# Attention and mixture of experts: a new opening order, chunk 1's scores in two banks, and idle products in other places

## The chip, the cores and the metric

The kernel runs on one core of a Trainium2 chip. The metric is device time in microseconds, the median of several runs of the whole program. Before the change it is 573.44 us (three runs, 573.29 to 575.0).

## The reference, cut to what matters

Eight batches of attention with keys and values pooled by 8, and behind it a two-level mixture of experts in which every token goes to one of 16 experts:

```python
k_p = k.reshape(B, H, Sp, pool, D).mean(axis=3)      # B=8, H=8, S=576, D=64, pool=8
v_p = v.reshape(B, H, Sp, pool, D).mean(axis=3)
scores = scale * np.matmul(q, k_p.transpose(0, 1, 3, 2))
scores = scores - np.max(scores, axis=-1, keepdims=True)
attn = np.exp(scores)
attn = attn / (np.sum(attn, axis=-1, keepdims=True) + 1e-09)
x = np.matmul(attn, v_p)                              # then (B*S, H*D)
# group of the token = argmax(x @ w_group), expert in the group = argmax(x @ w_expert[g])
h = np.maximum(x[tok] @ w1[g, e], 0.0)                # 512 -> 1024
out[tok] = (g_w * e_w)[:, None] * (h @ w2[g, e])      # 1024 -> 512
```

## The kernel before, in words

The work is done batch by batch. The attention of a batch (class Att) runs in five chunks of its 576 tokens (four of 128 and one of 64). The expert that most tokens of a batch choose is computed for all tokens of the batch (class Moe); tokens that chose another one are gathered and done at the end (class Left). All matrix products take fp32 data; the large ones run on a split into a rounded part and a rest, in three products.

The order of the work is written out by hand. Strings of pieces say what is issued one after another: START (line 34) and FIRST (line 44) for batch 0, STEADY for the batches after it, LAST for the last. A piece such as `a.sc:1` calls the method `sc` with 1; `a` is the attention of the current batch, `n` that of the next one, `x` that of the one after, `m` and `w` the experts of the current and the next batch, `t` the class Top. Each piece puts its instructions on the queues of the engines that it uses, and within one string each engine works through them in that order. The strings are run in separate blocks, START, then FIRST.

What START does, with the lines: `load_k`, `load_v`, `load_r`, `load_q` (185 to 211) load; `kr`, `rr`, `vr` (234 to 255) sum groups of 8 keys and values, on VectorE with the letter v (three additions) or r (one reduction, line 224), on GpSimd (POOL) with p. `kb` (248) is a copy on ScalarE (ACT), the first instruction there that needs the engine's table. `kt` (279) transposes the pooled keys on TensorE (PE), `kta` copies them out of PSUM. `qt` and `qta` transpose the queries of a chunk and copy them. `guess_x` (509) and `guess_e` (521) guess the expert of batch 0 from the mean of its values: two rounds of small products with a copy on ACT between them, then a chain on VectorE that ends at line 507, whose result SP reads into a register; the loads of that expert's weights (`m.load`, 576) are queued behind that. `split` (586) rounds a quarter of the weights on ACT, `spd` (593) forms the rest on POOL or VectorE.

A chunk's softmax is `sc` (scores on PE, line 335), `mx` (maximum, 341, VectorE), `sb` (difference, 348 in batch 0, 352 in later ones), `ex` (exponential, 357, ACT), `su_` (sum and reciprocal, VectorE), `nm` (multiplication, 372 and 375, POOL). `px_` and `pm` transpose the result on PE (380, 399), `pxa`, `pma`, `pxd`, `pmd` split it into a rounded part and a rest (404 on ACT, 408 on VectorE), `av` (410) multiplies by the values, `ava` and `avd` (420, 424) split that. `m.up:f:h` (597) is an up product of the expert, 12 products each, `ua` and `upd` (613, 618) its evacuation.

PSUM has eight banks here: three for up and down products and idle products (`ps_m`, tile "mm"), two that hold the scores of one chunk (`ps_s`, one tile), three for everything else (`ps_t`). `t.warm:z` (916) issues z idle products of 128x128 ones on PE into a bank of `ps_m`; nothing reads them. Each of them is two instructions in the profile.

The few lines that matter most, where a chunk's scores live and what an idle product is:

```python
ps = s.ss[c] = ps_s.tile([128, 2, 512], F32, name="sc")             # 329
ps = ps_m.tile([128, 512], F32, name="mm")                          # 918
for i in range(z):
    nc.tensor.matmul(ps[:, 0:128], lhsT=ones, rhs=ones, start=True, stop=True)   # 920
```

Of the kernel before, what the change touches and what calls it, by code (L numbers as in the profile page):

```python
# [33 lines left out]
START = """
a.load_r:v a.load_k:1:w a.kr:1:v t.warm:1 a.load_k:0:w t.load_wr a.load_v:0 a.kr:0:p t.warm:7 a.load_r:k a.load_v:1 a.load_q:0 a.vr:0:v a.rr:v
t.warm:11 a.load_q:1 t.warm:20 n.load_r:v a.kb a.vr:1:v a.kt n.load_r:k a.kta a.guess_x a.load_q:2 a.qt:0 a.qta:0 a.vmain a.guess_e a.sc:0 a.rcopy
m.load:1:1 a.qt:1 t.warm:2 a.vrem a.qta:1 a.qt:2 a.sc:1 a.mx:0 a.sb:0 a.ex:0 a.su_:0 a.nm:0:p a.mx:1 t.warm:4 a.vm:0 a.vrx a.sb:1 a.load_q:3 a.px_:0
m.load:1:3 a.pxa:0 a.vm:1 a.pm:0 a.pma:0 t.warm:1 t.warm:5 a.pxd:0 a.ex:1 a.pmd:0 a.av:1:0:128 a.av:2:0:128 m.load:1:2 a.av:0:0:128 a.su_:1 a.qta:2
a.ava:1:0:128 a.ava:2:0:128 a.ava:0:0:128 a.avd:1:0:128 a.avd:0:0:128 a.av:3:0:128 n.load_k:0 m.load:1:0 n.load_k:1 a.nm:1:p n.load_v:0 a.ava:3:0:128
m.split:1:1 a.sc:2 t.warm:1 a.pm:1 a.avd:3:0:128 a.load_q:4 a.mx:2 n.load_qb:2 a.px_:1 n.load_qb:0 a.qt:3 a.pxa:1 t.warm:3 a.avd:2:0:128 a.pma:1  # L40
a.sb:2 a.ex:2 a.pxd:1 m.split:1:0 a.pmd:1 m.spd:1:0:p a.su_:2 a.av:2:128:128 a.qta:3 a.ava:2:128:128 a.av:0:128:128 a.sc:3 n.load_qb:3 a.ava:0:128:128
a.av:1:128:128 a.av:3:128:128 a.ava:1:128:128 a.ava:3:128:128 a.avd:2:128:128 a.avd:0:128:128 a.avd:3:128:128 a.avd:1:128:128 m.up:0:0 m.spd:1:1:v
"""
FIRST = """
m.split:1:2 a.nm:2:p m.up:1:0 a.mx:3 m.ua:0:0 a.sb:3 n.vr:0 a.qt:4 a.px_:2 a.ex:3 a.su_:3 a.pm:2 m.ua:1:0 m.spd:1:2:p m.upd:0:0 a.qta:4 a.pxa:2 a.sc:4
a.mx:4 a.pma:2 a.sb:4 a.ex:4 a.pmd:2 m.up:2:0 m.split:1:3 t.warm:3 m.up:4:0 m.ua:2:0 a.nm:3:p m.load:2:1 a.pm:3 m.load:2:0 m.upd:1:0 a.px_:3 a.su_:4
a.nm:4:p m.ua:4:0 a.pxd:2 m.up:3:0 a.pxa:3 a.px_:4 a.pma:3 a.pxa:4 a.pxd:3 m.upd:2:0 a.pmd:3 a.pm:4 a.pxd:4 a.pma:4 m.split:2:1 a.pmd:4 a.av:3:256:320
a.av:2:256:320 m.upd:4:0 m.ua:3:0 a.ava:2:256:320 n.load_qb:1 x.load_k:0 a.ava:3:256:320 m.split:2:0 m.up:5:0 m.spd:1:3:v a.av:1:256:320 x.load_r:v
a.av:0:256:320 a.avd:2:256:320 a.ava:1:256:320 n.kr:0:r m.up:6:0 a.ava:0:256:320 a.avd:1:256:320 a.avd:3:256:320 m.ua:6:0 n.rr:p n.kr:1:p m.ua:5:0
m.spd:2:0:p m.load:2:2 a.avd:0:256:320 a.rt m.upd:3:0 m.upd:6:0 n.kt m.up:1:1 n.kta n.qb:0 m.upd:5:0 n.load_v:1 n.qb:1 n.sc:0 m.up:7:0 a.route  # L50
m.load:2:3 n.mx:0 n.rcopy n.sb:0 n.qb:2 m.ua:7:0 a.count n.ex:0 m.spd:2:1:p n.su_:0 m.ua:1:1 n.sc:1 n.nm:0:p m.up:0:1 n.mx:1 m.up:2:1 n.vrem m.ua:0:1
m.upd:7:0 a.gex n.sb:1 n.sc:2 m.upd:0:1 n.ex:1 m.upd:1:1 n.su_:1 n.px_:0 n.pm:0 n.mx:2 m.up:3:1 n.pxa:0 n.nm:1:p m.ua:2:1 m.up:4:1 x.load_k:1 m.ua:3:1
n.qb:3 n.px_:1 n.sb:2 x.load_qb:2 n.ex:2 n.pxd:0 x.load_r:k n.qb:4 m.split:2:2 m.upd:2:1 n.pxa:1 n.vrx a.gates n.pm:1 n.sc:3 n.vr:1:p n.mx:3 m.up:5:1
m.ua:4:1 m.up:7:1 n.vmain m.upd:3:1 n.pma:0 n.su_:2 n.nm:2:p m.up:6:1 a.keep_x m.ua:5:1 n.sb:3 m.upd:5:1 n.pm:2 n.px_:2 n.pxd:1 x.load_qb:3 x.load_v:0
n.sc:4 m.spd:2:2:p n.pmd:0 n.ex:3 n.vm:1 n.pma:1 m.upd:4:1 n.pmd:1 n.vm:0 n.pma:2 m.ua:6:1 m.ua:7:1 m.split:2:3 n.su_:3 n.nm:3:p n.pmd:2 n.av:1:0:256
n.mx:4 n.sb:4 x.load_qb:0 n.ava:1:0:256 n.pxa:2 n.px_:3 m.down:0 n.pxd:2 n.pm:3 m.down:1 n.av:0:0:256 n.ex:4 n.su_:4 x.load_qb:1 n.pxa:3 n.pma:3
n.pmd:3 n.nm:4:p n.pxd:3 m.upd:7:1 m.spd:2:3:p n.av:2:0:256 n.av:3:0:256 x.load_v:1 n.px_:4 n.ava:0:0:256 n.pm:4 n.avd:1:0:256 n.avd:0:0:256
n.ava:2:0:256 n.ava:3:0:256 n.avd:2:0:256 n.avd:3:0:256 n.pxa:4 m.down:2 n.pxd:4 n.pma:4 n.pmd:4 n.xr:3:0:256 n.av:0:256:320 n.av:1:256:320 x.kr:0:r
n.ava:0:256:320 n.av:3:256:320 n.ava:1:256:320 n.av:2:256:320 n.ava:3:256:320 n.xr:2:0:256 n.xr:1:0:256 n.xr:0:0:256 n.avd:0:256:320 n.ava:2:256:320
m.down:3 m.upd:6:1 n.avd:1:256:320 n.xr:1:256:320 n.avd:3:256:320 x.qb:0 n.xr:3:256:320 n.avd:2:256:320 n.xr:0:256:320 n.xr:2:256:320 m.da:0 m.down:4  # L60
n.rt m.down:5 x.rr:r n.route m.da:1 x.kr:1:p x.kt m.down:6 n.gex n.main_expert n.gates m.down:7 x.kta x.rcopy w.load:1:0 w.load:1:2 x.sc:0 x.mx:0
x.vrem x.vr:1:p w.load:1:3 m.down:8 m.down:9 w.split:1:0 x.vrx w.load:1:1 x.sb:0 x.qb:1 x.vr:0:r x.ex:0 m.down:12 x.su_:0 w.load:2:1 w.spd:1:0:v
n.keep_x m.down:13 x.nm:0:p m.down:10 m.da:2 w.split:1:1 m.da:4 m.down:11 x.vmain w.load:2:0 m.da:3 x.vm:1 w.spd:1:1:v x.vm:0
"""
# [907 lines left out]
```

## Time and profile before

| what | value |
|---|---|
| median of three runs | 573.44 us (573.29 to 575.0) |
| the profiled execution's own time | 573.03 us |
| its span | 571.3 us |
| mean granted clock of TensorE | 0.991 |
| busy share: PE, weight loads, VectorE, ACT, POOL | 98%, 87%, 70%, 48%, 53% |

PE is the engine of the matrix products, PEld its weight loads, which overlap with them. A line of a timeline names the start, the duration, the engine, the line of the kernel, the operation and its tiles; what stands in brackets is how long the engine had been idle and what ended that. `x4` means that four instructions are merged, and their duration runs from the first to the last. [...] START's pieces on PE run from the beginning to 35.39 us.

### The profile page before, as it was taken

How to read it: one execution, taken by the hardware profiler on the slowest of the kernel's cores; microseconds unless marked ns; L12 is line 12 of the kernel's file. 1: busy time of each engine (PE TensorE's matmuls, PEld its weight loads, DVE VectorE, ACT ScalarE, POOL GpSimd, SP SyncE). 2: the span in 40 equal slices, each digit the busy share in tenths (PEclk: the TensorE clock that was granted, in tenths of full speed). 3: DMA queues.
4: the chain of work that ended last, by engine and by line, in shares of the span. 5: the costliest groups of instructions: out<-in, count | busy, mean ns of one | idle time of the engine just before them, and what ended most of it. 6: DMA issues, size and time to landing. Idle time of an engine off the chain costs nothing. (4 is left out here: it accounts for less than half of the span.)

```text
span 571.3 us, 13094 instructions
## 1 busy us (share of the span) xinstructions
PE 558.4 (98%) x4896; PEld 497.5 (87%) x4896; DVE 397.1 (70%) x1075; ACT 273.8 (48%) x621; POOL 302.6 (53%) x301
## 2 busy tenths in 40 slices
PE   8999999999999999999999999999999999999995
...
GB/s 215 200 210 203 61 127 60 223 114 210 104 119 188 111 171 63 222 71 182 138 95 213 108 169 68 214 240 181 107 88 211 84 2 20 215 108 61 387 97 44
DMA packets 119362, 81.45 MB, mean 143 GB/s; under 512 B 76790, under 2 KB 95990, under 8 KB 118912
## 3 DMA queue, kind: packets, MB, share of 16 engines
...
q14 instruction: 26, 0.21, 0.1%
...
## 5 line engine op out<-in xcount | busy, mean ns | idle before, releaser
L608 PE MATMUL mm<-xt,w 128*128 128x320 f32 (+1 forms) x1536 | 221.1, 300 | 0.8 <-DVE ht L618 0.5
L608 PEld LDWEIGHTS mm<-xt,w 128*128 128x128 f32 x1536 | 208.2, 190 | 2.6 <-issue 0.7
L647 PE MATMUL mm<-w,ht 128*128 128x512 f32 x744 | 180.2, 395 | 0.0
L647 PEld LDWEIGHTS mm<-w,ht 128*128 128x128 f32 x744 | 136.9, 188 | 29.7 <-issue 1.8
L595 POOL TENSOR_TENSOR w<-sw,w 128x1024 fp32r<-128x1024 f32 x47 | 114.0, 2438 | 35.7 <-ACT w L590 35.7
L613 ACT ACTIVATE ht<-mm 128x320 fp32r<-128x320 f32 (+1 forms) x128 | 50.0, 410 | 62.1 <-PE mm L608 61.0
L618 DVE SCALAR_TENSOR_TENSOR ht<-mm,ht 128x256 fp32r<-128x256 f32 (+1 forms) x192 | 60.3, 347 | 25.0 <-ACT ht L613 24.2
L660 ACT ACTIVATE y<-mm,gm 128x512 f32<-128x512 f32 x31 | 21.2, 684 | 105.7 <-PE mm L647 105.7
L590 ACT CAST w<-sw 128x1024 fp32r<-128x1024 f32 x64 | 65.6, 1048 | 7.4 <-DMA sw<-in_moe_w_dram 7.3
L372 POOL TENSOR_TENSOR px<-p,su 128x128 f32<-128x128 f32 (+1 forms) x40 | 17.1, 427 | 68.0 <-DVE su L364 58.2
L272 POOL TENSOR_TENSOR rp<-rp,rh 32x128 f32<-32x128 f32 x8 | 3.6, 454 | 91.3 <-DMA rp<-rp 91.2
L431 POOL TENSOR_TENSOR sw<-xt 128x256 f32<-128x256 f32 (+1 forms) x56 | 43.7, 809 | 13.4 <-DVE xt L424 13.3
L375 POOL TENSOR_TENSOR p<-p,su 128x576 f32<-128x576 f32 (+1 forms) x40 | 46.0, 1150 | 3.1
L424 DVE TENSOR_TENSOR xt<-tp,xt 128x320 fp32r<-128x320 f32 (+2 forms) x68 | 28.1, 435 | 13.0 <-ACT xt L420 12.2
L420 ACT CAST xt<-tp 128x320 fp32r<-128x320 f32 (+2 forms) x68 | 25.4, 386 | 23.8 <-PE tp L417 22.5
L357 ACT ACTIVATE p<-p 128x576 f32<-128x576 f32 (+1 forms) x40 | 27.3, 682 | 16.4 <-DVE p L352 14.6
L362 DVE TENSOR_REDUCE su<-p 128x8 f32<-128x576 f32 (+1 forms) x40 | 29.8, 746 | 6.9 <-ACT p L357 6.0
L335 PEld LDWEIGHTS sc<-kT,qT 64*64 64x64 f32 x1264 | 24.1, 137 | 10.0 <-issue 4.8
L227 POOL TENSOR_TENSOR kv<-kv 128x512 f32<-128x512 f32 x20 | 32.5, 1627 | 0.2
L341 DVE TENSOR_REDUCE mx<-sc 128x8 f32<-128x576 f32 (+1 forms) x40 | 29.6, 741 | 3.4 <-PE sc L335 3.3
L335 PE MATMUL sc<-kT,qT 64*64 64x72 f32 x1264 | 30.1, 234 | 1.4 <-DVE p L352 1.0
L408 DVE TENSOR_TENSOR pl<-tp,ph 128x512 fp32r<-128x512 f32 (+1 forms) x40 | 25.2, 629 | 8.5 <-ACT ph L404 8.4
...
## 6 DMA issues: line engine op xcount, KB each, us to landing
...
```

The lines of the kernel that those rows point to most:

```text
L227: add(out=a[:, :, 0:256], in0=a[:, :, 0:256], in1=a[:, :, 256:512], op=ALU.add)
L335: nc.tensor.matmul(ps[t:t + 64, y, SP * g:SP * g + SP], lhsT=s.qT[c][r, g, t:t + 64], rhs=k, start=True, stop=True)
L341: red(out=mx[0:n], in_=scv, axis=AX.X, op=ALU.max)
L362: red(out=su[0:n], in_=s.p[c][0:n], axis=AX.X, op=ALU.add)
L375: eng.tensor_tensor(out=p[0:n], in0=p[0:n], in1=su[0:n].unsqueeze(3).broadcast_to([n, 2, 4, SP]), op=ALU.mult)
L431: nc.gpsimd.tensor_tensor(out=s.xw[g][:, sl], in0=s.xt[:, 0, g, sl].bitcast(F32), in1=s.xt[:, 1, g, sl].bitcast(F32), op=ALU.add)
L590: nc.scalar.copy(out=wh, in_=raw)
L595: (nc.vector if eng == "v" else nc.gpsimd).tensor_tensor(out=wl, in0=raw, in1=wh.bitcast(F32), op=ALU.subtract)
L608: nc.tensor.matmul(ps[:, 0:n], lhsT=l[:, kc, fs], rhs=xt[:, r, kc, sl], start=(kc == 0 and i == 0), stop=(kc == 3 and i == 2))
L613: nc.scalar.activation(out=s.ht[f][:, o:o + n], in_=s.pu[f, hf][:, 0:n], func=AF.Relu)
L618: stt(out=ht[:, at:at + hi - lo], in0=ps[:, lo - o:hi - o], scalar=0.0, in1=ht[:, lo:hi].bitcast(F32), op0=ALU.max, op1=ALU.subtract)
L647: nc.tensor.matmul(ps, lhsT=s.ht[f][:, 640 * l + o:640 * l + o + 128], rhs=s.w[2, f // 2][r][:, f % 2, :], start=(i == 0), stop=(i == 23))
```

## The change

START is a new list with the same pieces of attention and weights in another order, and two lines of FIRST differ. Beside the order:

- `t.prime` is new: a copy of one element on ACT at the head of its queue, in front of the five small loads that ACT issues.
- The scores of batch 0's chunk 1 (`a.sc:1:m`) go to two tiles of `ps_m`, one for each half of the scores, and `mx:1` and `sb:1` become two instructions each, one per half.
- `guess_e` stands behind `sc:0` and `mx:0`, ahead of `sb:0`; before it stood ahead of `sc:0`.
- The idle products: 55 in START before, 124 after. Ahead of `kt` there were 1+7+11+20 and now are 15+1+43+4+4; then 7 behind `kt`, 5 ahead of `sc:1`, 4+4+13 between `sc:1` and `px_:0`, 3+5 around `qt:2`, 4 behind `sc:2`, 7+1+4 around `qt:3`.
- `vr:0` is one reduction (letter r) instead of three additions; `n.load_k:0` is issued ahead of the `n.load_r`s; the loads of the weights come in the order 3, 2, 1, 0 instead of 1, 3, 2, 0.
- In FIRST: `a.su_:2` moves from START to its second place, `x.vr:0` goes from r to v, `w.spd:1:1` from VectorE to POOL.

The new START, the code for the scores in two tiles, and `prime`:

```diff
START = """
+t.prime t.warm:15 t.warm:1 t.warm:43 a.load_r:v a.load_k:1:w a.load_k:0:w t.load_wr a.load_v:0 a.load_r:k a.load_v:1 a.load_q:0 t.warm:4 a.kr:0:p
+a.load_q:1 a.kr:1:v t.warm:4 a.vr:0:r a.rr:v a.kb n.load_k:0 a.kt n.load_r:k a.kta t.warm:7 n.load_r:v a.qt:0 a.qta:0 a.load_q:2 a.vr:1:v a.guess_x
+a.sc:0 a.mx:0 a.guess_e a.sb:0 a.qt:1 m.load:1:3 t.warm:5 a.rcopy a.qta:1 a.vmain a.sc:1:m a.ex:0 a.mx:1 a.vm:0 t.warm:4 a.su_:0 a.sb:1 t.warm:4
+a.vm:1 a.nm:0:p m.load:1:2 t.warm:13 m.load:1:1 a.px_:0 a.pm:0 a.vrem a.ex:1 a.pxa:0 a.pma:0 a.su_:1 t.warm:3 a.qt:2 a.pxd:0 a.load_q:3 a.vrx t.warm:5
+m.load:1:0 a.pmd:0 a.av:1:0:128 a.nm:1:p n.load_v:0 a.av:2:0:128 a.av:0:0:128 a.qta:2 a.av:3:0:128 a.ava:1:0:128 a.avd:1:0:128 a.ava:0:0:128 a.sc:2
+a.avd:0:0:128 t.warm:4 a.ava:3:0:128 a.ava:2:0:128 m.split:1:1 a.avd:2:0:128 a.pm:1 a.mx:2 a.px_:1 a.pxa:1 a.pma:1 t.warm:7 a.qt:3 a.avd:3:0:128
+t.warm:1 a.load_q:4 a.sb:2 n.load_k:1 n.load_qb:2 n.load_qb:0 a.pxd:1 a.ex:2 m.split:1:0 t.warm:4 m.spd:1:0:p a.pmd:1 a.av:2:128:128 a.qta:3
+a.av:0:128:128 a.sc:3 a.ava:2:128:128 a.av:1:128:128 a.av:3:128:128 a.avd:2:128:128 n.load_qb:3 a.ava:0:128:128 a.ava:1:128:128 a.avd:0:128:128
+a.ava:3:128:128 a.avd:3:128:128 a.avd:1:128:128 m.up:0:0 m.spd:1:1:v
 """
...
@@ -324,24 +326,39 @@
             s.qT[c] = sm.tile([128, NG, 128], F32, name="qT")
             nc.vector.transpose(out=s.qT[c][:, :, 0:n], in_=s.q[:, 0:NG * S].rearrange("p (g t) -> p g t", g=NG)[:, :, o:o + n])
 
-        def sc(s, c):
+        def sc(s, c, home="s"):
             n = s.span(c)[1]
-            ps = s.ss[c] = ps_s.tile([128, 2, 512], F32, name="sc")
+            if home == "m":
+                s.ss[c] = ps = [ps_m.tile([128, 512], F32, name="mm") for y in range(2)]
+            else:
+                s.ss[c] = ps_s.tile([128, 2, 512], F32, name="sc")
+                ps = [s.ss[c][:, y] for y in range(2)]
             for g in range(NG):
                 for t in range(0, n, 64):
                     for y in range(2):
                         r = slice(64 * y, 64 * y + 64)
                         k = s.kT[r, g // 2, SP * (g % 2):SP * (g % 2) + SP] if s.b else s.kT[r, g, 0:SP]
-                        nc.tensor.matmul(ps[t:t + 64, y, SP * g:SP * g + SP], lhsT=s.qT[c][r, g, t:t + 64], rhs=k, start=True, stop=True)
+                        nc.tensor.matmul(ps[y][t:t + 64, SP * g:SP * g + SP], lhsT=s.qT[c][r, g, t:t + 64], rhs=k, start=True, stop=True)
 
         def mx(s, c):
             n = s.span(c)[1]
+            if type(s.ss[c]) is list:
+                s.m[c] = sm.tile([128, 2, 4], F32, name="mx")
+                for y in range(2):
+                    red(out=s.m[c][0:n, y], in_=s.ss[c][y][0:n, 0:288].rearrange("p (x s) -> p x s", s=SP), axis=AX.X, op=ALU.max)
+                return
             scv = s.ss[c][0:n, :, 0:288].rearrange("p u (x s) -> p u x s", s=SP)
             mx = s.m[c] = sm.tile([128, 2, 4], F32, name="mx")
             red(out=mx[0:n], in_=scv, axis=AX.X, op=ALU.max)
 
         def sb(s, c):
             n = s.span(c)[1]
+            if type(s.ss[c]) is list:
+                p = s.p[c] = sm.tile([128, 2, 4, SP], F32, name="p")
+                for y in range(2):
+                    tt(out=p.rearrange("p u x s -> p (u x) s").rearrange("p (g y) s -> p y g s", y=2)[0:n, y],
+                       in0=s.ss[c][y][0:n, 0:288].rearrange("p (x s) -> p x s", s=SP), in1=bc(s.m[c][0:n, y], SP), op=ALU.subtract)
+                return
             scv, mx = s.ss[c][0:n, :, 0:288].rearrange("p u (x s) -> p u x s", s=SP), s.m[c]
             p = s.p[c] = sm.tile([128, 2, 4, SP], F32, name="p")
             if not s.b:
@@ -913,6 +930,9 @@
             for g in range(G):
                 nc.scalar.dma_start(out=wr[:, :, 4 + 4 * g:8 + 4 * g], in_=we[g].rearrange("(c p) e -> p c e", p=128))
 
+        def prime(s):
+            nc.scalar.copy(out=gate[0:1, 0, 0:1], in_=ones[0:1, 0:1])
+
         def warm(s, z):
 
             ps = ps_m.tile([128, 512], F32, name="mm")
```

## Rows read from the trace of the kernel before

**Rows 1.** Busy time by stretch: length, then each engine's busy us (instructions), PEclk, DMA, GB/s.
```profile
1.00:5.00 4.00, 3.85 (x18) 3.86 (x19) 1.40 (x11) 0.00 (x0) 2.57 (x19) 1.00 0.65 177
...
15.30:22.05 6.75, 6.66 (x81) 6.07 (x84) 3.57 (x12) 3.74 (x10) 1.18 (x2) 0.50 0.36 92
...
35.00:95.00 60.00, 56.76 (x605) 50.57 (x605) 55.25 (x142) 35.48 (x89) 42.07 (x42) 1.00 0.50 123
...
95.00:500.00 405.00, 405.00 (x3452) 360.33 (x3451) 285.34 (x758) 202.44 (x459) 226.99 (x212) 1.00 0.49 140
```

**Rows 2.** Timeline, front of START: start, us, engine, line, operation, out<-in, count [idle before].
```profile
1.15 10.81 PE L920 MATMUL mm<-ones 128*128 128x128 f32 x78 [1.15 <-DVE valid L125]
...
9.04 1.05 POOL L232 TENSOR_TENSOR kb<-w 128x256 f32<-128x256 f32 x1
...
10.62 1.28 ACT L250 ACT_TABLE_LOAD   x1 [10.62 <-DMA wr<-in_moe_w_expert_dram]
...
11.69 0.47 PEld L290 LDWEIGHTS tp<-ident,kb 128*128 128x128 f32 x4
...
12.24 0.40 ACT L250 COPY rp<-rp 32x256 f32<-32x256 f32 x1 [0.34 <-DVE rp L232]
...
12.69 0.21 PEld L293 LDWEIGHTS tp<-ident,rp 128*128 128x128 f32 x2 [0.53 <-ACT rp L250]
```

**Rows 3.** Timeline, the guess and chunk 0's scores; last, a pair of 288-element subtractions.
```profile
13.06 0.20 PEld L514 LDWEIGHTS tp<-sel,vp 128*64 128x64 f32 x4 [0.16 <-DVE kv L227]
...
14.71 0.42 PEld L314 LDWEIGHTS tp<-ident,q 128*128 128x128 f32 x4
...
15.46 1.90 PE L525 MATMUL tp<-wr,ht 128*128 128x20 f32 x8
...
17.28 1.24 PE L335 MATMUL sc<-kT,qT 64*64 64x72 f32 x32
...
18.58 0.22 DVE L507 TENSOR_SCALAR moh<-cr,ct 128x16 f32<-128x16 f32 x1
...
19.50 0.76 DVE L348 TENSOR_TENSOR p<-sc,mx 128x576 f32<-128x576 f32 x1
...
20.29 0.68 ACT L357 ACTIVATE p<-p 128x576 f32<-128x576 f32 x1
...
61.47 0.82 DVE L352 TENSOR_TENSOR p<-sc,mx 128x288 f32<-128x288 f32 x2
```

**Rows 4.** Timeline, chunk 0 from its weights to its values.
```profile
22.86 1.15 POOL L375 TENSOR_TENSOR p<-p,su 128x576 f32<-128x576 f32 x1
...
24.06 0.42 PEld L399 LDWEIGHTS tp<-ident,p 128*128 128x128 f32 x4 [0.76 <-POOL p L375]
...
25.95 0.69 DVE L408 TENSOR_TENSOR pl<-tp,ph 128x512 fp32r<-128x512 f32 x1 [0.96 <-ACT ph L404]
...
26.69 0.19 PEld L417 LDWEIGHTS tp<-pl,vmh 128*128 128x128 f32 x1 [0.43 <-DVE pl L408]
```

**Rows 5.** Timeline, from chunk 2's scores to the first up product.
```profile
28.54 0.58 PEld L335 LDWEIGHTS sc<-kT,qT 64*64 64x64 f32 x32
...
29.57 0.42 PEld L399 LDWEIGHTS tp<-ident,p 128*128 128x128 f32 x4
...
33.38 2.36 POOL L595 TENSOR_TENSOR w<-sw,w 128x1024 fp32r<-128x1024 f32 x1 [3.86 <-ACT w L590]
...
34.64 0.76 DVE L341 TENSOR_REDUCE mx<-sc 128x8 f32<-128x576 f32 x1 [0.17 <-PE sc L335]
...
35.39 3.10 PEld L608 LDWEIGHTS mm<-xt,w 128*128 128x128 f32 x24
...
36.17 0.48 DVE L424 TENSOR_TENSOR xt<-tp,xt 128x128 fp32r<-128x128 f32 x2
```

**Rows 6.** Timeline, an up product behind an idle product in FIRST.
```profile
42.78 0.19 PEld L608 LDWEIGHTS mm<-xt,w 128*128 128x128 f32 x1 [0.25 <-PE mm L920]
...
42.95 0.41 DVE L618 SCALAR_TENSOR_TENSOR ht<-mm,ht 128x256 fp32r<-128x256 f32 x1
```

More of the change, by code (lines that the diff above doesn't have):

```diff
@@ L34 @@
 START = """
[L35 to L42, printed above, removed]
+t.prime t.warm:15 t.warm:1 t.warm:43 a.load_r:v a.load_k:1:w a.load_k:0:w t.load_wr a.load_v:0 a.load_r:k a.load_v:1 a.load_q:0 t.warm:4 a.kr:0:p
@@ L43 @@
 """
 FIRST = """
[L45 to L60, printed above, removed]
@@ L61 @@
-n.rt m.down:5 x.rr:r n.route m.da:1 x.kr:1:p x.kt m.down:6 n.gex n.main_expert n.gates m.down:7 x.kta x.rcopy w.load:1:0 w.load:1:2 x.sc:0 x.mx:0
-x.vrem x.vr:1:p w.load:1:3 m.down:8 m.down:9 w.split:1:0 x.vrx w.load:1:1 x.sb:0 x.qb:1 x.vr:0:r x.ex:0 m.down:12 x.su_:0 w.load:2:1 w.spd:1:0:v
-n.keep_x m.down:13 x.nm:0:p m.down:10 m.da:2 w.split:1:1 m.da:4 m.down:11 x.vmain w.load:2:0 m.da:3 x.vm:1 w.spd:1:1:v x.vm:0
+m.split:1:2 a.su_:2 a.nm:2:p m.up:1:0 a.mx:3 m.ua:0:0 a.sb:3 n.vr:0 a.qt:4 a.px_:2 a.ex:3 a.su_:3 a.pm:2 m.ua:1:0 m.spd:1:2:p m.upd:0:0 a.qta:4
@@ new lines @@
+a.pxa:2 a.sc:4 a.mx:4 a.pma:2 a.sb:4 a.ex:4 a.pmd:2 m.up:2:0 m.split:1:3 t.warm:3 m.up:4:0 m.ua:2:0 a.nm:3:p m.load:2:1 a.pm:3 m.load:2:0 m.upd:1:0
+a.px_:3 a.su_:4 a.nm:4:p m.ua:4:0 a.pxd:2 m.up:3:0 a.pxa:3 a.px_:4 a.pma:3 a.pxa:4 a.pxd:3 m.upd:2:0 a.pmd:3 a.pm:4 a.pxd:4 a.pma:4 m.split:2:1
+a.pmd:4 a.av:3:256:320 a.av:2:256:320 m.upd:4:0 m.ua:3:0 a.ava:2:256:320 n.load_qb:1 x.load_k:0 a.ava:3:256:320 m.split:2:0 m.up:5:0 m.spd:1:3:v
+a.av:1:256:320 x.load_r:v a.av:0:256:320 a.avd:2:256:320 a.ava:1:256:320 n.kr:0:r m.up:6:0 a.ava:0:256:320 a.avd:1:256:320 a.avd:3:256:320 m.ua:6:0
@@ new lines @@
+n.rr:p n.kr:1:p m.ua:5:0 m.spd:2:0:p m.load:2:2 a.avd:0:256:320 a.rt m.upd:3:0 m.upd:6:0 n.kt m.up:1:1 n.kta n.qb:0 m.upd:5:0 n.load_v:1 n.qb:1 n.sc:0
+m.up:7:0 a.route m.load:2:3 n.mx:0 n.rcopy n.sb:0 n.qb:2 m.ua:7:0 a.count n.ex:0 m.spd:2:1:p n.su_:0 m.ua:1:1 n.sc:1 n.nm:0:p m.up:0:1 n.mx:1 m.up:2:1
+n.vrem m.ua:0:1 m.upd:7:0 a.gex n.sb:1 n.sc:2 m.upd:0:1 n.ex:1 m.upd:1:1 n.su_:1 n.px_:0 n.pm:0 n.mx:2 m.up:3:1 n.pxa:0 n.nm:1:p m.ua:2:1 m.up:4:1
+x.load_k:1 m.ua:3:1 n.qb:3 n.px_:1 n.sb:2 x.load_qb:2 n.ex:2 n.pxd:0 x.load_r:k n.qb:4 m.split:2:2 m.upd:2:1 n.pxa:1 n.vrx a.gates n.pm:1 n.sc:3
@@ new lines @@
+n.vr:1:p n.mx:3 m.up:5:1 m.ua:4:1 m.up:7:1 n.vmain m.upd:3:1 n.pma:0 n.su_:2 n.nm:2:p m.up:6:1 a.keep_x m.ua:5:1 n.sb:3 m.upd:5:1 n.pm:2 n.px_:2
+n.pxd:1 x.load_qb:3 x.load_v:0 n.sc:4 m.spd:2:2:p n.pmd:0 n.ex:3 n.vm:1 n.pma:1 m.upd:4:1 n.pmd:1 n.vm:0 n.pma:2 m.ua:6:1 m.ua:7:1 m.split:2:3 n.su_:3
+n.nm:3:p n.pmd:2 n.av:1:0:256 n.mx:4 n.sb:4 x.load_qb:0 n.ava:1:0:256 n.pxa:2 n.px_:3 m.down:0 n.pxd:2 n.pm:3 m.down:1 n.av:0:0:256 n.ex:4 n.su_:4
+x.load_qb:1 n.pxa:3 n.pma:3 n.pmd:3 n.nm:4:p n.pxd:3 m.upd:7:1 m.spd:2:3:p n.av:2:0:256 n.av:3:0:256 x.load_v:1 n.px_:4 n.ava:0:0:256 n.pm:4
@@ new lines @@
+n.avd:1:0:256 n.avd:0:0:256 n.ava:2:0:256 n.ava:3:0:256 n.avd:2:0:256 n.avd:3:0:256 n.pxa:4 m.down:2 n.pxd:4 n.pma:4 n.pmd:4 n.xr:3:0:256
+n.av:0:256:320 n.av:1:256:320 x.kr:0:r n.ava:0:256:320 n.av:3:256:320 n.ava:1:256:320 n.av:2:256:320 n.ava:3:256:320 n.xr:2:0:256 n.xr:1:0:256
+n.xr:0:0:256 n.avd:0:256:320 n.ava:2:256:320 m.down:3 m.upd:6:1 n.avd:1:256:320 n.xr:1:256:320 n.avd:3:256:320 x.qb:0 n.xr:3:256:320 n.avd:2:256:320
+n.xr:0:256:320 n.xr:2:256:320 m.da:0 m.down:4 n.rt m.down:5 x.rr:r n.route m.da:1 x.kr:1:p x.kt m.down:6 n.gex n.main_expert n.gates m.down:7 x.kta
@@ L64 @@
+x.rcopy w.load:1:0 w.load:1:2 x.sc:0 x.mx:0 x.vrem x.vr:1:p w.load:1:3 m.down:8 m.down:9 w.split:1:0 x.vrx w.load:1:1 x.sb:0 x.qb:1 x.vr:0:v x.ex:0
+m.down:12 x.su_:0 w.load:2:1 w.spd:1:0:v n.keep_x m.down:13 x.nm:0:p m.down:10 m.da:2 w.split:1:1 m.da:4 m.down:11 x.vmain w.load:2:0 m.da:3 x.vm:1
+w.spd:1:1:p x.vm:0
 """
```

## Prediction

> **What bounds the kernel now.** I read busy time by stretch first. From 95 to 500 us the engine of the matrix products (PE) is busy 405.00 of 405 us, and from 35 to 95 us 56.76 of 60 [rows 1]. So the body has almost no slack on PE: whatever delays its first up product (m.up:0:0, which begins at 35.39 us [rows 5]) delays the end, and only the 3.24 us that PE lacks between 35 and 95 us could take some of it up. The changed list, START, is all that lies ahead of 35.39. There I read the timeline in the order of the work: pooled keys and values, their transposes (kt, line 290), the guess of the expert, scores, softmax, attention values, first up product.
>
> [...] (a) PE starts with idle products at 1.15 us; 39 of them are 78 instructions, and only when they are through does the first transpose of kt begin, at 11.69 us [rows 2]. Its input, POOL's kb, was done at 10.09; the second part waits for a copy that ends at 12.64 [rows 2]. The front of idle products therefore ended about when kt's inputs were there. [...] (c) From there the chain is one of small steps over all engines, and PE takes its instructions in the order of the list.
>
> **The idle products in front.** The new list has 15+1+43+4+4 = 67 idle products ahead of kt instead of 39. The pace: 78 instructions between 1.15 and 11.69; the first 18 end at 5.00, so 60 take 6.69 us, 0.1115 each, 0.223 per product [rows 1, 2]. The added 28 cost 28 x 0.223 = 6.24 us, and nothing hides them, because PE itself is what kt then waits for: 11.69+6.24 = 17.93. The transposes need 0.47+0.21, now without the wait for the copy, so they are issued by 18.61; before it was 12.90 [rows 2]: **+5.71**.
>
> **Edits ahead of kt** end in the same answer. The table load (1.28 us, at 10.62 [rows 2]) goes to the front of ScalarE; the copy after it waited for VectorE's sum until 12.2 anyway, and now it has to be there only by 18. vr:0 as one reduction, the new order of the loads, and n.load_k:0 moved ahead of the n.load_r's on SP also end before 17.93: their gain is 0, and a loss of up to 17.93-12.64 = 5.3 us would stay hidden.
>
> **kt to the scores.** Before, sc:0 started 17.28-12.90 = 4.38 us after kt [rows 2, 3]. Now: 7 idle products 1.56, qt:0 0.42, guess_x 14.71-13.06 = 1.65 [rows 3], together 3.63 at the full clock: sc:0 at 22.25, **+4.97**. The guess now ends behind the scores: its second part starts 0.75 us after guess_x's end (15.46-14.71 [rows 3]), at 23.0; it took 1.90 at 0.50, so 0.95 at full clock; VectorE's chain to the end of L507 ran from 17.36 to 18.80 = 1.44 [rows 3], so 25.4. sb:0 stands behind that chain on VectorE although its scores and maxima have been ready since about 24: 25.4 against 19.50, **+5.9**. The reordering costs this 0.9. On SP the read of the guess holds up what is queued behind it, the four loads of w1, q3 and n.load_v:0, by 25.4-18.8 = 6.6 us. They would be issued from about 26.4; split:1:0 needs the last at 39.4 and qt:3 its q3 at 38.8, so 12 us are left and nothing waits. If the loads took all of that, each further us would go straight into spd:1:0.
>
> **Chunk 1 in two banks.** sc:1 need no longer wait for sb:0; PE issues guess_e's last product 0.1 ahead of its result, at 23.85, then qt:1 (0.42) and five idle products (1.12): sc:1 runs from 25.4 to 26.0 (0.58, as sc:2 [rows 5]). But its maxima stand behind sb:0 on VectorE (26.2), so this is worth nothing there. mx:1 and sb:1 become two instructions each over half the elements. No row shows this; the nearest, two subtractions of 288 elements, take 0.82 against 0.76 for one of 576 [rows 3]. Bounds are 0.76 and 1.52 for a pair; I take 0.82, the nearest row. mx:1 ends at 27.0, 0.1 after ex:0 (26.2+0.68), so it holds up su_:0 by 0.1; at the upper bound by 0.8. [...] The row of the pair shows 0.06 and decides.
>
> From ex:0's start to the end of nm:0 it was 24.01-20.29 = 3.72 [rows 3, 4]; now 26.2+3.72+0.1 = 30.0. But PE has 4+4+13 = 21 idle products in its queue ahead of px:0 and pm:0: 26.0+21x0.223 = 30.7, plus 0.11, so pm:0 is issued at 30.8 against 24.06: **+6.75**, 0.75 of it new.
>
> **pm:0 to the first up product.** Three idle products, qt:2 and five more stand between pm:0 (0.42) and av: 0.42+0.67+0.42+1.12 = 2.63, av at 33.4. The old interval from pm:0 to the product that waits for pl was 26.69-24.06 = 2.63 [rows 4] with two products of 0.11 ahead of it; here that product comes at 33.6, **+6.95**, and pl (by 33.2: the old steps without the vm:1 that lay in them) does not bind. Sixteen value products need 1.8: sc:2 at 35.2 instead of 28.54 [rows 5], **+6.65**. Then sc:2 0.58, four idle products 0.89, pm:1 at 36.7 (before 29.57 [rows 5]), **+7.1**; its nm:1 has been done since about 33, so chunk 1's lead of 3 us ends in PE's queue. pm:1 and px:1 0.53, 7 idle 1.56, qt:3 0.42, 5 idle 1.12: av for columns 128 on at 40.3. Two groups 0.9, sc:3 0.6, two groups 0.9: m.up:0:0 at **42.7 instead of 35.39**. POOL's spd:1:0 [rows 5] would end at about 42.9 behind split:1:0, the same lateness as PE. That is **+7.3 us**.
>
> After that every engine stands to m.up:0:0 as before. su_:2, moved to FIRST, is no loss: VectorE took mx:3 of FIRST at 34.64 ahead of START's last avd at 36.17 [rows 5], so a piece at the head of FIRST fills a gap in START. If it does not, it stands behind spd:1:1, and POOL's chain of FIRST loses up to 4 us: upper end. x.vr:0 and w.spd:1:1 lie where PE is always busy [rows 1]: 0.
>
> **Sum.** The profiled execution took 573.03 (span 571.3, 1.73 around it); +7.3 = 580.3. The median of the runs is 0.41 higher, so **580.8**.
>
> **Rivals.** *Banks.* After sc:1, two of the three banks of the up products hold scores until sb:1 has read them (first half 28.6). If the second group of idle products gets one of those, PE stands from 26.9 to 28.7: +1.8, 582.6. Against it: m.up:4:0 waited for an idle product and started at 42.78, before upd:1:0 (42.95) had freed the oldest bank [rows 6], so a bank just left by an idle product is given out again.
> *The clock falls again.* Before, it fell after kt, guess_x and qt:0 [rows 1, 3]; the same stretch comes at 20.2 to 24, though with idle products on both sides and no wait in it. If it runs at 0.50 for 6.75 us again, PE loses half of that, 3.4, and pm:0 hangs on PE: 584.2.
> *Not slower.* PE takes idle products only in gaps, as VectorE took mx:3 early. Then kt ends at 12.9, sc:0 starts at 15.0, the guess ends at 18.15, sb:0 starts 1.35 ahead of 19.50, and pm:1 need no longer wait for a late nm:1: about 1.7 us gained in all, 571.7. It decides if kt starts before about 12 us. Against it: the 78 instructions all ran ahead of kt although its input was there at 10.09 [rows 2].
>
> **Numbers.** Forecast 0.62 (own range 578.5 to 582.5, from closing part of the 3.24 us to 0.8 at mx:1 and some of FIRST), banks 0.12, clock 0.20, not slower 0.06. The range 577.5 to 585.5 leaves out the last and the worst sums of two. 0.3% (1.7 us) is what a measurement tells from no change: slower 0.94, within 0.03, faster 0.03.
>
> **What would show it.** 134 idle instructions ahead of L290, and L290 at about 18; sb:0 behind L507; idle products right up to pm:0; granted clock 1.00 at 15 to 22; m.up:0:0 at about 42.7, and from there the old distances. It is wrong if L290 starts near 12, or if m.up:0:0 is late and the end is not.

## The result and the profile after

The changed kernel takes **582.27 us** in the median (five runs, 581.8 to 583.53), beside 573.44 for the kernel before in the same set (573.29 to 575.55): a ratio of 1.0146, interval 1.0123 to 1.0169. By that ratio it is 8.4 us slower; the medians are 8.8 apart. The profiled execution took 582.72 us, with a span of 581.0 and a mean granted clock of 0.998 (all clocks here are shares of TensorE's full clock). The code after has other line numbers: idle products L940, kt L292 and L295, sc L341, mx L348 and L352, sb L359 and L365, the guess's second part L542, its result L524, nm L392, pm L416, split L607, spd L612, up L625.

Busy time by stretch, with the columns of [rows 1]:

```profile
15.30:22.05 6.75, 6.75 (x70) 6.52 (x68) 0.00 (x0) 1.45 (x4) 0.00 (x0) 1.00 0.40 76
15.00:45.00 30.00, 29.87 (x373) 28.57 (x373) 13.84 (x38) 14.88 (x37) 7.02 (x8) 1.00 0.53 142
44.60:104.60 60.00, 56.85 (x605) 50.81 (x604) 54.91 (x142) 35.32 (x89) 42.01 (x42) 1.00 0.53 126
95.00:500.00 405.00, 404.55 (x3459) 359.98 (x3458) 289.74 (x768) 202.91 (x464) 233.78 (x219) 1.00 0.48 134
```

Where the clock had been 0.50 (15.30 to 22.05 us [rows 1]) it is now 1.00, and PE is busy 29.87 of 30 us up to the first up product: the opening is nothing but PE's queue. The 60 us behind that product look as before, 56.85 against 56.76 [rows 1], so the body is moved, not changed.

The front of the timeline, to lay beside [rows 2]:

```profile
0.82 1.28 ACT L934 ACT_TABLE_LOAD   x1 [0.82 <-PEq L978]
...
1.14 17.41 PE L940 MATMUL mm<-ones 128*128 128x128 f32 x134 [1.14 <-DVE valid L127]
...
12.70 0.40 ACT L252 COPY rp<-rp 32x256 f32<-32x256 f32 x1 [10.39 <-DVE rp L234]
...
18.28 0.47 PEld L292 LDWEIGHTS tp<-ident,kb 128*128 128x128 f32 x4
...
18.72 0.25 PEld L295 LDWEIGHTS tp<-ident,rp 128*128 128x128 f32 x2
```

134 instructions run without a break, and kt begins behind the last, at 18.28 instead of 11.69, though the copy that it needs was done at 13.10. Then the scores and the guess, beside [rows 3]:

```profile
22.79 0.58 PEld L341 LDWEIGHTS sc<-kT,qT 64*64 64x64 f32 x32
...
23.53 0.97 PEld L542 LDWEIGHTS tp<-wr,ht 128*128 128x128 f32 x8 [0.16 <-ACT ht L536]
...
23.59 0.76 DVE L352 TENSOR_REDUCE mx<-sc 128x8 f32<-128x576 f32 x1 [9.41 <-PE sc L341]
...
25.83 0.23 DVE L524 TENSOR_SCALAR moh<-cr,ct 128x16 f32<-128x16 f32 x1
25.96 0.75 DVE L365 TENSOR_TENSOR p<-sc,mx 128x576 f32<-128x576 f32 x1
26.13 0.58 PEld L341 LDWEIGHTS mm<-kT,qT 64*64 64x64 f32 x32
...
26.79 0.97 PEld L940 LDWEIGHTS mm<-ones 128*128 128x128 f32 x8
...
26.91 0.82 DVE L348 TENSOR_REDUCE mx<-mm 128x4 f32<-128x288 f32 x2 [0.19 <-PE mm L341]
...
28.00 0.97 PEld L940 LDWEIGHTS mm<-ones 128*128 128x128 f32 x8 [0.25 <-PE mm L940]
...
28.75 0.77 DVE L359 TENSOR_TENSOR p<-mm,mx 128x288 f32<-128x288 f32 x2
...
29.22 2.98 PEld L940 LDWEIGHTS mm<-ones 128*128 128x128 f32 x26 [0.25 <-PE mm L940]
29.46 1.15 POOL L392 TENSOR_TENSOR p<-p,su 128x576 f32<-128x576 f32 x1
...
32.23 0.47 PEld L416 LDWEIGHTS tp<-ident,p 128*128 128x128 f32 x4
```

Chunk 0's weights are ready at 30.61 (29.46+1.15), and their transposes pm:0 start at 32.23, behind the last of the 21 idle products. The groups of 4, 4 and 13 are apart by 0.25 us each: scores hold two of the three banks, so each group waits for the one before it to leave the third. From there, beside [rows 5]:

```profile
36.83 0.58 PEld L341 LDWEIGHTS sc<-kT,qT 64*64 64x64 f32 x32
...
38.38 0.47 PEld L416 LDWEIGHTS tp<-ident,p 128*128 128x128 f32 x4
...
41.28 0.74 DVE L379 TENSOR_REDUCE su<-p 128x8 f32<-128x576 f32 x1
...
42.23 2.37 POOL L612 TENSOR_TENSOR w<-sw,w 128x1024 fp32r<-128x1024 f32 x1 [8.96 <-ACT w L607]
...
44.63 3.06 PEld L625 LDWEIGHTS mm<-xt,w 128*128 128x128 f32 x24
```

The first up product comes at 44.63 instead of 35.39, +9.24; the span is longer by 9.7. su_:2 (L379), the piece moved to FIRST, fills a gap inside START at 41.28.

### The profile page after: what moved, and what is told of

Its sections match the earlier page's. It is cut to its first block, busy times and chain, and to the rows that moved or that the text cites. A ratio compares the mean times of both kernels' runs of the same rounds, so it can differ in the third digit from the quotient of the medians.

```text
span 581.0 us, 13368 instructions
## 1 busy us (share of the span) xinstructions
PE 569.7 (98%) x5034; PEld 510.5 (88%) x5034; DVE 395.5 (68%) x1076; ACT 274.4 (47%) x622; POOL 304.6 (52%) x302
## 5 line engine op out<-in xcount | busy, mean ns | idle before, releaser
L625 PE MATMUL mm<-xt,w 128*128 128x320 f32 (+1 forms) x1536 | 221.1, 300 | 1.0 <-DVE ht L635 0.7
L625 PEld LDWEIGHTS mm<-xt,w 128*128 128x128 f32 x1536 | 208.1, 190 | 3.0 <-DVE ht L635 1.2
L612 POOL TENSOR_TENSOR w<-sw,w 128x1024 fp32r<-128x1024 f32 x48 | 116.3, 2438 | 40.6 <-ACT w L607 40.6
L607 ACT CAST w<-sw 128x1024 fp32r<-128x1024 f32 x64 | 65.6, 1049 | 7.9 <-DMA sw<-in_moe_w_dram 7.9
L392 POOL TENSOR_TENSOR p<-p,su 128x576 f32<-128x576 f32 (+1 forms) x40 | 46.0, 1150 | 3.1
L352 DVE TENSOR_REDUCE mx<-sc 128x8 f32<-128x576 f32 (+1 forms) x39 | 28.9, 741 | 12.6 <-PE sc L341 12.5
L437 ACT CAST xt<-tp 128x320 fp32r<-128x320 f32 (+2 forms) x68 | 25.4, 386 | 24.5 <-PE tp L434 23.1
L379 DVE TENSOR_REDUCE su<-p 128x8 f32<-128x576 f32 (+1 forms) x40 | 29.9, 749 | 7.5 <-ACT p L374 6.3
L940 PE MATMUL mm<-ones 128*128 128x128 f32 x254 | 33.0, 289 | 1.3 <-DVE valid L127 1.1
L940 PEld LDWEIGHTS mm<-ones 128*128 128x128 f32 x254 | 31.5, 204 | 1.8 <-DVE valid L127 1.1
L341 PEld LDWEIGHTS sc<-kT,qT 64*64 64x64 f32 x1232 | 22.7, 133 | 9.2 <-issue 4.8
```

The source lines that it names most:

```text
L379: red(out=su[0:n], in_=s.p[c][0:n], axis=AX.X, op=ALU.add)
L392: eng.tensor_tensor(out=p[0:n], in0=p[0:n], in1=su[0:n].unsqueeze(3).broadcast_to([n, 2, 4, SP]), op=ALU.mult)
L607: nc.scalar.copy(out=wh, in_=raw)
L612: (nc.vector if eng == "v" else nc.gpsimd).tensor_tensor(out=wl, in0=raw, in1=wh.bitcast(F32), op=ALU.subtract)
L625: nc.tensor.matmul(ps[:, 0:n], lhsT=l[:, kc, fs], rhs=xt[:, r, kc, sl], start=(kc == 0 and i == 0), stop=(kc == 3 and i == 2))
```

## The experiments

Each ratio is to the runs of the kernel before in the same set; their medians lie between 573.4 and 575.2. A difference between two kernels of different sets is therefore taken from their ratios. The table takes from one profile of each kernel when the weight load of kt begins, the distance from there to that of pm:0, from that to the first up product, and from that to the end of the span (us).

| run | ratio, 95% interval | kt | kt to pm:0 | pm:0 to up | up | up to end |
|---|---|---|---|---|---|---|
| before | 1 | 11.69 | 12.37 | 11.33 | 35.39 | 535.9 |
| after | 1.0146 (1.0123 to 1.0169) | 18.28 | 13.95 | 12.40 | 44.63 | 536.4 |
| front39 | 1.0057 (1.0031 to 1.0084) | 11.86 | 15.78 | 12.41 | 40.05 | 536.1 |
| no_mid21 | 1.0159 (1.0135 to 1.0184) | 17.72 | 12.39 | 14.83 | 44.94 | 536.0 |
| front39_no_mid21 | 1.0074 (1.0047 to 1.0101) | 11.30 | 14.64 | 15.02 | 40.96 | 537.1 |
| before_front67 | 1.0101 (1.0077 to 1.0126) | 17.70 | 11.56 | 10.96 | 40.22 | 536.5 |
| no_banks | 1.0153 (1.0134 to 1.0173) | 17.75 | 14.04 | 12.41 | 44.20 | 536.3 |
| guess_first | 1.0172 (1.0149 to 1.0194) | 18.43 | 14.72 | 12.41 | 45.56 | 536.6 |
| sb0_first | 1.0148 (1.0127 to 1.0169) | 17.57 | 13.95 | 12.41 | 43.93 | 535.9 |
| no_prime | 1.0141 (1.0114 to 1.0169) | 17.59 | 13.95 | 12.40 | 43.94 | 536.2 |
| early | 1.0009 (0.9991 to 1.0027) | 10.89 | 12.36 | 11.93 | 35.18 | 537.3 |
| early2 | 1.0033 (1.0014 to 1.0051) | 10.81 | 15.54 | 12.10 | 38.45 | 537.4 |
| early3 | 1.0005 (0.9988 to 1.0022) | 11.13 | 10.49 | 13.08 | 34.70 | 536.9 |
| early4 | 1.0006 (0.9992 to 1.0020) | 10.87 | 11.37 | 12.37 | 34.61 | 537.5 |

**front39: the 28 added front products taken out of the new kernel.**

```diff
-t.prime t.warm:15 t.warm:1 t.warm:43 a.load_r:v
+t.prime t.warm:15 t.warm:1 t.warm:15 a.load_r:v
```

> The changed kernel with 31 instead of 59 idle products at the head, so 39 ahead of the key transposes (kt) as before. Theory (the front of idle products is what delays kt, and kt starts the path to the first up product): 28 x 0.223 = 6.2 us come off PE's front; kt's second part then waits for the copy that ended at 13.1 us, so 5.5 us are saved: about 576.8 us, still above the kernel before by some 3 us. Rival A (the late guess, and with it the weights' loads, sets the first up product): less than 2 us saved, 580.5 or more. Rival B (the added idle products only kept the clock up): it falls again at about 15 to 22 us and eats 2 to 3 us of the saving, 579.

The time is 577.67 us. The ratio is 0.0089 below that of the change, about 5.1 us, near the 5.5 of the theory. In the profile kt is back at 11.86, 6.42 earlier, but the first up product is only 4.58 earlier. The windows of this run (columns as above) show where the rest went:

```profile
15.00:19.00 4.00, 3.99 (x71) 3.71 (x71) 1.17 (x4) 1.18 (x3) 0.00 (x0) 1.00 0.77 128
19.00:21.00 2.00, 2.00 (x14) 1.77 (x16) 1.42 (x6) 1.36 (x3) 0.72 (x1) 0.51 0.00 0
21.00:23.00 2.00, 2.00 (x39) 1.86 (x40) 0.88 (x3) 1.99 (x6) 0.00 (x0) 0.64 0.47 141
```

The granted clock falls to 0.51 (19 to 21 us) after the guess's small products, as in rival B though later and by less, and kt to pm:0 is 15.78 instead of 13.95. This holds for the profiled execution, whose mean granted clock is 0.993. Four of the run's nine executions have a mean of 0.998 to 0.999, as high as the changed kernel's, and take 576.2 to 576.7 us, the 576.8 of the theory. So the front products always cost their time in the queue, and gave a part of it back as clock only in those executions in which the clock would have fallen.

**no_mid21 and front39_no_mid21: the 4+4+13 idle products out, alone and with the front's 28.**

```diff
-... a.mx:1 a.vm:0 t.warm:4 a.su_:0 a.sb:1 t.warm:4
-a.vm:1 a.nm:0:p m.load:1:2 t.warm:13 m.load:1:1 a.px_:0 a.pm:0
+... a.mx:1 a.vm:0 a.su_:0 a.sb:1
+a.vm:1 a.nm:0:p m.load:1:2 m.load:1:1 a.px_:0 a.pm:0
```

> The changed kernel without the 4+4+13 idle products between chunk 1's scores and chunk 0's transposed weights. Theory: pm:0 waits for POOL's nm:0 (ended 30.61 us) instead of the products (issued 32.34), 1.7 us saved: 580.6 us. Rival (these products hold the clock): with PE idle from 26.7 to 29.4 us the clock falls to 0.50, what follows is up to 3 us slower: 582 to 584 us.

> Both cuts together, 39 idle products ahead of kt and none between chunk 1's scores and chunk 0's transposed weights. Theory: 5.5 + 1.7 = 7.2 us saved, 575.1 us, about 1.6 us above the kernel before, which is the order's own cost (the subtraction of chunk 0 behind the guess, idle products further on). Rival (the clock falls once PE has gaps): 577 to 579.

The times are 583.22 and 579.6 us: no gain, against my theory and as the rivals had it (the second lies 0.6 us above its rival's range). In no_mid21 pm:0 is 1.56 us earlier behind kt (12.39), then all of it is lost (14.83 instead of 12.40). Its windows, and pm:0 in its timeline:

```profile
27.00:29.00 2.00, 0.11 (x1) 0.12 (x1) 1.90 (x6) 1.77 (x5) 0.50 (x2) 0.87 0.74 223
29.00:35.00 6.00, 5.25 (x24) 4.96 (x25) 2.38 (x6) 3.11 (x8) 3.07 (x4) 0.50 1.04 316
```

```profile
28.88 0.18 PEld L397 LDWEIGHTS tp<-ident,px 128*128 128x128 f32 x1 [2.73 <-POOL px L389]
...
30.11 0.71 PEld L416 LDWEIGHTS tp<-ident,p 128*128 128x128 f32 x4 [1.04 <-POOL p L392]
```

PE stands for 2.73 and 1.04 us, and the stretch from 29 to 35 us runs at 0.50. Without the 21 products kt to up is 27.22 instead of 26.35 (with the short front 29.66 instead of 28.19): they delay pm:0 and pay for it by the clock. All five executions of no_mid21 have a mean clock of 0.991 or 0.992, where the changed kernel's have 0.998 or 0.999. With both cuts one execution of eight kept 0.998 and took 575.36 us, near the 575.1 of the theory; the other seven lie at 0.987 to 0.993 and take 578.0 to 580.5. The ratios of each pair overlap, so the times alone show only that nothing is gained by leaving them out.

**before_front67: the 28 front products alone, in the kernel before.**

```diff
-t.warm:11 a.load_q:1 t.warm:20 n.load_r:v a.kb
+t.warm:11 a.load_q:1 t.warm:48 n.load_r:v a.kb
```

> The kernel before with 28 more idle products ahead of kt and nothing else. Theory: 28 x 0.223 = 6.2 us of delay less the 1.0 us that kt's second part waited for the copy, and nothing takes it up later: 573.4 + 5.5 = 578.9 us. If the clock then stays at 1.00 from 15 to 28 us, up to 2 us of that come back: 577. Rival (the front costs nothing as such, the new order does): within 1 us of the kernel before, 573 to 574.5.

The time is 579.66 us and the ratio 1.0101, that is 5.8 us, near the theory's figure and 5 us above the rival's. kt is 6.01 later and the first up product 4.83; shorter waits and a shorter slow stretch (0.65 and 0.50 from 21 to 25 us, where it was 0.50 from 15.30 to 22.05 [rows 1]) take up the rest. The clock did not stay at 1.00 here, although all 67 products ran ahead of kt:

```profile
21.00:23.00 2.00, 2.00 (x32) 1.96 (x36) 0.54 (x3) 1.19 (x3) 0.72 (x1) 0.65 0.07 16
23.00:25.00 2.00, 2.00 (x24) 1.86 (x19) 1.85 (x6) 0.45 (x1) 0.45 (x1) 0.50 0.00 0
```

So from both sides the front explains some 5 to 6 of the 8.4 us.

**no_banks, sb0_first, guess_first, no_prime: single edits undone in the new kernel.**

```diff
-a.sc:1:m
+a.sc:1
...
-a.sc:0 a.mx:0 a.guess_e a.sb:0 a.qt:1
+a.sc:0 a.mx:0 a.sb:0 a.guess_e a.qt:1
...
-a.sc:0 a.mx:0 a.guess_e a.sb:0 a.qt:1
+a.guess_e a.sc:0 a.mx:0 a.sb:0 a.qt:1
...
-t.prime t.warm:15 t.warm:1
+t.warm:15 t.warm:1
```

> The changed kernel with chunk 1's scores back in the scores' own two banks, in one tile. Theory (PE's queue of idle products, not chunk 1's softmax, sets the next step): sc:1 waits for sb:0 (ended 26.71 us), so it starts 0.65 us later than 26.13, and the idle products and pm:0 behind it on PE by the same: +0.65 us, 582.9 us. Rival (the two banks are what the change gains, chunk 1's chain being critical): +2 us or more, 584.5.

The time is 582.77 us, near the theory's 582.9 and far from the rival's 584.5. But the theory's mechanism holds only for sc:1: its lateness does not reach pm:0. Two rows of the timeline show that two effects cancel:

```profile
26.34 0.73 PE L341 MATMUL sc<-kT,qT 64*64 64x72 f32 x32 [0.66 <-DVE p L365]
```

```profile
27.00 4.76 PEld L940 LDWEIGHTS mm<-ones 128*128 128x128 f32 x42
```

In the scores' own banks sc:1 waits 0.66 us for sb:0 to leave them; but then the 21 idle products run as one stream of 42 instructions in 4.76 us, where the changed kernel's three groups take 5.41 (26.79 to 32.20) with their two breaks of 0.25. kt to pm:0 is 14.04 against 13.95, 0.09 longer and not 0.65; a difference of that size the times cannot show.

> The changed kernel with chunk 0's difference ahead of the guess's chain on VectorE. It can start at 24.4 instead of 25.96 us, and the guess ends 0.5 later. Theory (21 idle products stand between chunk 1's scores and pm:0, so PE's queue hides it): within 1 us of the changed kernel, 581.5 to 582.8. Rival (VectorE's chain sets pm:0): 1.5 us saved, 580.8 or less.

The time is 582.53 us, and kt to pm:0 is 13.95, the same to the hundredth: sb:0 behind the guess costs nothing while PE's queue ends last.

> The changed kernel with the guess's second part ahead of chunk 0's scores, as it was. My step said that the late guess costs 0.9 us on chunk 0's difference; by that this gives 581.4 us. Rival: PE then stands 0.8 us waiting for ScalarE's copy between the two parts of the guess, and scores, maxima and difference all come about 0.8 us later: 583.1 us, so that the reordering was a gain of its own.

The time is 583.86 us: here my step was wrong in sign, and the rival right. kt to pm:0 is 14.72, 0.77 longer, because PE waits for ACT's copy between the guess's two parts and has no scores to put there:

```profile
23.69 1.07 PE L542 MATMUL tp<-wr,ht 128*128 128x20 f32 x8 [0.68 <-ACT ht L536]
...
24.69 0.73 PE L341 MATMUL sc<-kT,qT 64*64 64x72 f32 x32
```

The ratios of the two kernels overlap, so the times alone do not show the 0.77; the profile does.

> The changed kernel without the copy that loads ScalarE's table first. Theory (the copy of the keys' remainder waits for VectorE's sum until 12.4 us, and kt for PE until 18.3): no change, 581.8 to 582.8 us. Rival (the table load lies on the path): +1.3 us, 583.6.

The time is 582.5 us: no effect, as the theory had it. The table load is back ahead of the copy, as in [rows 2], and both are long done when kt begins at 17.59:

```profile
10.77 1.28 ACT L252 ACT_TABLE_LOAD   x1 [10.77 <-DMA wr<-in_moe_w_expert_dram]
...
12.89 0.40 ACT L252 COPY rp<-rp 32x256 f32<-32x256 f32 x1 [0.84 <-DVE rp L234]
```

**early to early4: can the change's good parts win with a short front?** They put chunk 0's scores ahead of the whole guess, keep the two banks, and have 31 idle products (early) or 35 (the others) in front, kb on VectorE instead of ACT, the last loads that kt and qt:0 need ahead of the values' loads, and FIRST as it was before.

```diff
-t.prime t.warm:15 t.warm:1 t.warm:43 a.load_r:v ... a.vr:0:r a.rr:v a.kb n.load_k:0 a.kt
+t.prime t.warm:15 t.warm:16 a.load_r:v ... a.rr:v a.kb:v a.vr:0:v a.vr:1:v a.kt
...
-a.guess_x a.sc:0 a.mx:0 a.guess_e a.sb:0 a.qt:1 ... a.sc:1:m
+a.sc:0 a.mx:0 a.sb:0 a.qt:1 ... a.guess_x a.su_:0 a.sc:1:m a.mx:1 t.warm:2 a.guess_e
```

> A new opening, with FIRST as in the kernel before: 31 idle products in front, the remainder of the keys and q0 loaded ahead of the values, the keys' copy on VectorE, chunk 0's and chunk 1's scores ahead of the guess, idle products only where PE would wait. Theory (the start of kt plus the chain behind it sets the first up product): kt can start at about 10.1 us, sc:0 at 12.6, pm:0 at 19 against 24.06 in the kernel before, the first up product at about 30 against 35.4: 568 us. Rival A (the weights' loads set it): they start at about 20 us, the last needed one lands by 25, split and rest end by 31: 570. Rival B (the clock falls in the gaps): 571 to 573.

The time is 574.15 us: no difference from before, and not the gain expected. kt to pm:0 was 12.36, with the clock at 0.68 in 17 to 19 us and 0.50 from 19 to 23: the clock fell, as in rival B. early2 has 4 more products in front and 7 more from there to sc:1, further loads issued earlier, and vmain ahead of guess_x:

> The new opening again, mended by what its trace showed: the next batch's keys and values and the later queries are loaded while the DMA queue waited for the guess (idle from 18 to 29 us), their remainders behind them, vr:1 on POOL, idle products where PE stood idle or ran only the guess's small products, and the guess's second part behind chunk 1's scores and four idle products. Theory (kt's start and the chain behind it, at the full clock, set the first up product): the clock stays at 1.00, pm:0 at about 20.3 us, first up product at about 32 against 35.4, 570 us. Rival A (the clock falls again once the guess runs): 573 or more, as the first try. Rival B (the opening's lead is given back in FIRST, whose loads come no earlier): first up product at 32 but 572 to 573 us in all.

The time is 577.15 us, slower than before. One row of its timeline gives the cause:

```profile
18.14 0.20 PEld L531 LDWEIGHTS tp<-sel,vp 128*64 128x64 f32 x4 [2.18 <-POOL vp L262]
```

The guess reads values that vmain changes on POOL, so guess_x stood behind that piece; PE waited 2.18 us, and the clock was 0.50 from 19 to about 29 us. early3 tests this: it exchanges the two pieces, early4 adds four idle products behind qt:2:

```diff
-a.vmain a.guess_x a.su_:0 a.sc:1:m a.mx:1 a.qt:2 t.warm:4 a.sb:1
+a.guess_x a.vmain a.su_:0 a.sc:1:m a.mx:1 a.qt:2 t.warm:4 a.sb:1     (early3)
+a.guess_x a.vmain a.su_:0 a.sc:1:m a.mx:1 a.qt:2 t.warm:8 a.sb:1     (early4)
```

> The opening of the run early2 with one piece moved: vmain stands behind guess_x instead of ahead of it. In early2 guess_x waited on PE from 15.95 to 18.14 us for POOL's subtraction, PE stood, and the granted clock fell to 0.50. Theory: guess_x starts at about 16.1, its 24 products run at the full clock, the granted clock stays at 1.00 until 20, sc:1 is at about 18 instead of 20.28, pm:0 at about 21 instead of 26.35, the weights' loads go out at about 23, up:0:0 is at 33 to 34 instead of 36 or more, and the time is 2 to 4 us below early2's (571 to 574 where the kernel before takes 573.5 to 575). Rival: the small products of the guess (a single column each) let the clock fall by themselves, as in the kernel before at 15.3; then the clock is 0.50 from about 17 to 23, pm:0 is at 23 to 24 and the time is equal to the run early, within 0.3% of the kernel before.

> early3 with 8 instead of 4 idle products between chunk 2's query transposes and the second part of the guess. Theory that idle products bridge a stretch: if the clock falls in early3 behind sc:1, this one holds it at 1.00 there and is 0.5 to 1.5 us faster than early3. If the clock falls already in the guess's small products, or does not fall, the 4 added products are 0.9 us in PE's queue ahead of the guess's end and of chunk 0's weights, and this run is equal to early3 or up to 0.9 us slower.

The times are 573.87 and 574.07 us beside 573.56 for the kernel before: no difference. The theory of early3 held up to pm:0 and failed behind it. Two windows of early3, and one wait of its timeline with the same wait before:

```profile
15.00:25.00 10.00, 9.28 (x115) 8.49 (x113) 6.07 (x19) 6.09 (x14) 3.01 (x5) 1.00 0.90 225
35.00:95.00 60.00, 56.17 (x599) 49.91 (x599) 55.03 (x141) 34.89 (x88) 39.62 (x39) 1.00 0.50 114
```

```profile
62.06 0.73 PE L341 MATMUL sc<-kT,qT 64*64 64x72 f32 x32 [1.24 <-DVE p L369]
```

```profile
62.44 0.73 PE L335 MATMUL sc<-kT,qT 64*64 64x72 f32 x32 [1.03 <-DVE p L352]
```

The clock stays at 1.00, pm:0 comes at 21.62 against 24.06 [rows 4], 2.44 earlier. Of that 1.75 is lost by the first up product (13.08 instead of 11.33), and 0.69 is left. At the wait shown 0.38 is left (62.06 against 62.44): PE came to it earlier and waited 0.21 longer. From 35 to 95 us PE is busy 56.17 instead of 56.76 [rows 1], and the span ends no earlier, 571.6 beside 571.3. In early4 the clock was 1.00 too, so the four products had nothing to hold. kt to pm:0 is 0.88 longer, about the 0.89 that four cost; but pm:0 to the first up product is 0.71 shorter, so by there PE would have waited anyway and they cost nothing.

## Why the prediction was right in its direction and cause, and 1.5 us short

**The front** held. All 67 products run before kt and nothing hides them: kt begins at 18.28, forecast 17.93. Six profiled executions with this list and front begin kt between 17.57 and 18.43, so the forecast lies inside their spread and the profiled execution near its late end. Both directions of the experiment agree (5.1 and 5.8 us), and the rival *not slower* fell with the 134 unbroken instructions.

**kt to the scores**: sc:0 began at 22.79 (forecast 22.25) and sb:0, behind L524, at 25.96 (25.4), both late by about what the front was and 0.2 more. **The reordering costs 0.9** is the step that failed: sb0_first shows that sb:0's lateness is not on the path, and guess_first that the new place of the guess saves PE 0.77. The sum did not rest on this step: pm:0 was taken from PE's queue (30.7), not from sb:0's chain (30.0). **The pairs on half the elements** cost 0.82 and 0.77, close to the row that I chose. The groups by line and form (count, then busy us and mean ns) tell more than the pairs do:

```profile
L352 DVE TENSOR_REDUCE mx<-sc 128x8 f32<-128x576 f32 x38 | 28.1, 741 | 12.6 <-PE sc L341 12.5
...
L348 DVE TENSOR_REDUCE mx<-mm 128x4 f32<-128x288 f32 x2 | 0.8, 452 | 0.2 <-PE mm L341 0.2
...
L365 DVE TENSOR_TENSOR p<-sc,mx 128x576 f32<-128x576 f32 x3 | 2.3, 753 | 0.1
...
L359 DVE TENSOR_TENSOR p<-mm,mx 128x288 f32<-128x288 f32 x2 | 0.8, 427 | 0.0
```

One half of the maximum alone takes 452 ns against 741 for the whole, so by a straight line through these two sizes an estimated 163 ns of each do not depend on the size (2x452-741); for the difference it is 101 (2x427-753). But the two halves overlap, and the pair of maxima is 0.82, not 0.90.

**The 21 idle products** are the largest term that was mis-sized: from sc:1 to pm:0 it took 6.10 us instead of 5.4. Of the 0.70, 0.50 are PE's idle time at the two handovers of one bank; beside the unbroken stream of no_banks the handovers cost 0.65 (5.41 less 4.76). I had asked whether a group would wait for the banks of the scores (the rival *banks*, which fell: no such wait is there) and not whether groups confined to one bank wait for each other. That rival's time, 582.6, lies nearer to the measured 582.27 than my 580.8: the time alone would have spoken for it, and only the timeline decides against it.

**pm:0 to the first up product** took 12.40 instead of 11.9, in small steps, all in PE's queue. So the first up product is +9.24 instead of +7.3: 0.35 more in the front, 0.19 up to sc:0, 0.19 to sc:1, 0.70 and 0.50. Behind it 0.45 more came in, of the size by which the distance from there to the end differs between executions (535.9 to 536.6 in the kernels with this list and front). Almost nothing (0.09) was taken up by the 3.24 us that PE lacks between 35 and 95: the shift was rigid.

**The clock** stayed at 1.00, as forecast, so the rival *the clock falls again* fell for this kernel. But the forecast valued idle products only by their time in the queue; no_mid21 and front39 show that they can also pay: 21 of them back in full, the front's 28 with 1.83 us (15.78 less 13.95) of their 6.42 in the profiled execution, and with nothing where the clock held without them, as it did by the mean clock in four of front39's nine executions.

What stays open is, first, the rest of the 8.4 us. front39, with the old front, is still slower than the kernel before (1.0057, some 3 us). Behind kt the new list has 57 idle products instead of 16, by the forecast's 0.223 an estimated 9.1 us more of queue, and kt to the first up product is 2.65 us longer (26.35 against 23.70). Only the 21 were taken out by themselves, so what the others cost or pay is not shown. Open is also which of the waits between pm:0 and 95 us keeps an earlier opening from becoming a shorter kernel. In early3 the guess ends 3.7 us later than before (22.53 against 18.80) and the loads of the weights start that much later; a version with both early was not run.
